# Turned activations laid out sign by sign, in a fused FNet and SoLU kernel on one Trainium2 core

## The chip, the cores and the metric

The kernel runs on one core of one Trainium2 chip. The metric is the device time of one execution in microseconds (us), as a median of several. Before the change it is 1179.93 us (three executions, 1179.46 to 1180.57 us). The profile comes from one execution more, whose span from first to last instruction is 1174.4 us.

Five engines work beside each other: TensorE (PE in the profile; its weight loads are PEld), VectorE (DVE), ScalarE (ACT), GpSimd (POOL) and SyncE (SP), which here does nothing but issue DMA transfers. All tiles named below lie in SBUF with 128 partitions, but for those with `ps` in their name, which lie in PSUM. All arithmetic is in fp32.

## The reference

Eight sequences of 3136 tokens with 256 features go through a two-dimensional Fourier transform, of which the real part is kept. Its rows then go through a feed-forward block with 1024 hidden features.

```python
def _attn_ref(x):                       # x: 8 x 3136 x 256
    X = np.fft.fft(x, axis=1)
    X = np.fft.fft(X, axis=2)
    return X.real.astype(np.float32)

def _moe_ref(x, w_in, w_out, g_ln):     # x: 25088 x 256
    h = x @ w_in                        # 25088 x 1024
    e = np.exp(h - np.max(h, axis=-1, keepdims=True))
    sm = e / (np.sum(e, axis=-1, keepdims=True) + 1e-09)
    solu = h * sm
    mu = np.mean(solu, axis=-1, keepdims=True)
    var = np.mean((solu - mu) ** 2, axis=-1, keepdims=True)
    ln = (solu - mu) / np.sqrt(var + 1e-06) * g_ln
    return ln @ w_out                   # 25088 x 256
```

## The kernel before

The transform over tokens is split as 3136 = 49 x 64. The eight sequences are taken as four pairs, and a pair gives 25 **units**, one for each `k1`. A unit holds 128 tokens of each of two **signs** (`s` = 0 and 1; the tokens of one sign mirror those of the other, and `k1` = 0 has one sign alone). So there are 100 units, numbered 0 to 99.

A unit goes through these steps. `transform2` makes `q` on TensorE, and ScalarE copies it to SBUF. `spread` takes one row of `q` as a column `r`, by a small DMA. `up` multiplies `q` by the weights into PSUM, `even` (VectorE, reads `r`) and `join` make the hidden rows of both signs, and `expo`, `product` and `square` make `u`, which is 128 tokens x 1024 features for each sign. `u` must be transposed, because in the last product its features lie along the partitions. For units 0 to 3 TensorE does that (`turn_whole`). For all later ones VectorE transposes blocks of 32 x 32 into `v` (`turn_blocks`), and DMA moves the blocks to their places in `uT` (`move_blocks`): 16 transfers for two units together, each from 32 partitions to 32 partitions. `down` multiplies `uT` by `Wo`, where 128 x 128 of `uT` are the weights that TensorE loads. For odd units seven products of half-size blocks replace the eight (`Down`, `sums`, `product7`); their sums `S` come from GpSimd. The DMA of the results to `out` ends the unit.

```python
qpool = ctx.enter_context(tc.tile_pool(name="qpool", bufs=4))          # q
...
def spread(t):
    t.r = small.tile([P, 1], FP32, tag="r", name="r")
    nc.sync.dma_start(out=t.r, in_=t.q[0:1, P : 2 * P])
...
class Batch:                            # two units: w = 0 and 1
    def __init__(self, by_blocks):
        if by_blocks:
            self.v = fpool.tile([P, 2, FF, 2], FP32, tag="v", name="v32", bufs=2)
        self.uT = fpool.tile([P, 2, KF, 4, 64], FP32, tag="uT", name="uT", bufs=2)

def turn_blocks(t, s):
    for o in (s,) if len(t.signs) == 2 else (0, 1):
        nc.vector.transpose(out=t.batch.v[:, t.w, :, o], in_=t.u[s])
...
def move_blocks(batch, units, engines=(nc.sync,)):
    v = batch.v[:, units].rearrange("p w (c q n) s -> p q (w c) (n s)", q=4, n=32)
    uT = batch.uT[:, units].rearrange("p w c i m -> p i (w c) m")
    for i in range(4):
        for q in range(4):
            a, b = slice(32 * i, 32 * i + 32), slice(32 * q, 32 * q + 32)
            engines[i % len(engines)].dma_start(out=uT[b, i], in_=v[a, q])
...
def blocks(t):                          # the four blocks of the seven products
    uT = t.batch.uT[:, t.w].rearrange("p c i (n s) -> p s c (i n)", s=2)
    return [uT[:, s, c : c + KF // 2] for s in range(2) for c in (0, KF // 2)]
...
def product7(o, a, b, start=False):
    n = KF // 2
    for c in range(n):
        nc.tensor.matmul(o, a[:, c], b[:, c], start=start and c == 0, stop=c == n - 1, ...)
...
def down(t, s, ps=None):                # the plain product of one sign
    uT = t.batch.uT[:, t.w].rearrange("p c i (n s) -> p c (i n) s", s=2)
    ...
    for c in range(KF):
        nc.tensor.matmul(ps, uT[:, c, :, s], Wo[:, c, :], start=(c == 0), stop=(c == KF - 1))
```

In `v` and `uT` the two signs of a token stand side by side: the value of sign 0, then that of sign 1. A row of 32 tokens of both signs is a run of 64 values, which is 256 bytes, and every reader of one sign steps over the other.

The loop over units, cut to what the change touches. Sums and products of unit `i - lag` stand in step `i`, with `lag` = 4 and `whole` = 4:

```python
for i in range(whole + 1, len(units) + lag + 3):
    cur = units[i] ...                  # fills this step
    old = units[i - lag] ...            # is multiplied by Wo in this step
    kept = units[i - lag - 3] ...       # is stored in this step
    if seven: sums(old)
    ...
    for s in kept.signs: store(kept, s)             # sign 0 by SyncE, sign 1 by GpSimd
    ...
    even(cur, up(cur, 0))
    cur.odd = up(cur, 1)
    second_transform(i + 2)                         # transform2, copy to q, spread
    for s in cur.signs: join(cur, s)
    ...                                             # products of old, expo, product, square
    for s in cur.signs: turn_blocks(cur, s)
    if i >= len(units) - 2:
        move_blocks(batches[-1], slice(cur.w, cur.w + 1), (nc.sync, nc.gpsimd) if cur.w else (nc.sync,))
    elif cur.w:
        move_blocks(batches[-1], slice(0, 2))       # once in two steps
    ...
    if cur.p == 0 and i in (5, 8, 11):
        turn(first, (i + 1) // 3)                   # loads g, which transform2 reads
    for pr in pairs[1:]:
        turn_parts(pr, i - pr.p * NK)               # the same for the next pair
```

Of the kernel before, what the change touches and what calls it, by code (L numbers as in the profile page):

```python
# [9 lines left out]
FP32 = mybir.dt.float32  # L10
# [7 lines left out]
P = 128  # L18
# [17 lines left out]
def kernel(  # L36
# [19 lines left out]
    nc = tc.nc  # L56
    B, S, D = x.shape
    FF = moe_w_in.shape[1]
    KF = FF // P
# [9 lines left out]
    xpool = ctx.enter_context(tc.tile_pool(name="xpool", bufs=2))  # L69
    zpool = ctx.enter_context(tc.tile_pool(name="zpool", bufs=2))  # L70
    gpool = ctx.enter_context(tc.tile_pool(name="gpool", bufs=3))
    qpool = ctx.enter_context(tc.tile_pool(name="qpool", bufs=4))
    small = ctx.enter_context(tc.tile_pool(name="small", bufs=7))
    dram = ctx.enter_context(tc.tile_pool(name="dram", bufs=2, space=bass.MemoryType.DRAM))
    ps_h = ctx.enter_context(tc.tile_pool(name="ps_h", bufs=1, space=PSUM))
# [8 lines left out]
    Wo = const.tile([P, KF, D], FP32, name="Wo")  # L84
# [208 lines left out]
    class Batch:  # L293


        def __init__(self, by_blocks):
            if by_blocks:
                self.v = fpool.tile([P, 2, FF, 2], FP32, tag="v", name="v32", bufs=2)
            self.uT = fpool.tile([P, 2, KF, 4, 64], FP32, tag="uT", name="uT", bufs=2)

    def turn_blocks(t, s):

        for o in (s,) if len(t.signs) == 2 else (0, 1):
            nc.vector.transpose(out=t.batch.v[:, t.w, :, o], in_=t.u[s])  # L304

    def turn_whole(t):

        uT = t.batch.uT[:, t.w].rearrange("p c i (n s) -> p c (i n) s", s=2)
        n = KF // 2
        t.wait = []  # L310
        for s in t.signs:
            for half in range(2):
                ps = result(2 * s + half + 1).rearrange("p (c k) -> p c k", c=n)
                for c in range(n):
                    f = half * n + c
                    nc.tensor.matmul(ps[:, c, :], t.u[s][:, f * P : (f + 1) * P], ident, is_transpose=True,
                                     start=(c == 0), stop=(c == n - 1), skip_group_check=True)
                if s:
                    t.wait.append((uT[:, half * n : (half + 1) * n, :, s], ps))
                else:  # L320
                    nc.scalar.copy(uT[:, half * n : (half + 1) * n, :, s], ps)  # L321

    def move_blocks(batch, units, engines=(nc.sync,)):

        v = batch.v[:, units].rearrange("p w (c q n) s -> p q (w c) (n s)", q=4, n=32)
        uT = batch.uT[:, units].rearrange("p w c i m -> p i (w c) m")
        for i in range(4):
            for q in range(4):
                a, b = slice(32 * i, 32 * i + 32), slice(32 * q, 32 * q + 32)
                engines[i % len(engines)].dma_start(out=uT[b, i], in_=v[a, q])  # L330
# [11 lines left out]
            nc.gpsimd.tensor_tensor(out=Ws[:, j], in0=a, in1=b, op=ALU.subtract)  # L342

    def blocks(t):
        uT = t.batch.uT[:, t.w].rearrange("p c i (n s) -> p s c (i n)", s=2)
        return [uT[:, s, c : c + KF // 2] for s in range(2) for c in (0, KF // 2)]

    def sums(t):

# [86 lines left out]

    def down(t, s, ps=None):

        uT = t.batch.uT[:, t.w].rearrange("p c i (n s) -> p c (i n) s", s=2)
        if ps is None:  # L440
            ps = (result(0) if s else bank(0))[:, 0:D]
        for c in range(KF):
            nc.tensor.matmul(ps, uT[:, c, :, s], Wo[:, c, :], start=(c == 0), stop=(c == KF - 1))  # L443
        return ps

    def scale(t, s, ps):
# [188 lines left out]

    def turn_parts(pr, step):

        at = (-4 if pr.p == 1 else -5, -3, 2, 6, 11)
        if step in at:
            turn(pr, at.index(step))  # L640

    with tc.manual_schedule():
# [102 lines left out]
        def other_pairs(i, do, *a):  # L745
            cur = units[i]
            if cur.p + 1 < NP:
                do(pairs[cur.p + 1], i, *a)
# [3 lines left out]
        for i in range(whole + 1):  # L752
            cur = units[i]
            prv = units[i - 1] if i else None
            if prv:
                turn_whole(prv)
            for s in cur.signs:
                join(cur, s)
            if prv:
                for o, ps in prv.wait:  # L760
                    nc.vector.tensor_copy(out=o, in_=ps)
            for s in cur.signs:
                expo(cur, s)
            if i == whole:
                ps_o = down(units[0], 0)
            if i == 0:

                weights.narrow_out(3)
            for s in cur.signs:
                product(cur, s)  # L770
                if i < whole and s == 0:
                    square(cur, s)
            if i == 1:
                weights.centre()
                weight_sums()
            if i < whole:

                begin(i + 1)
                if 1 in cur.signs:
                    square(cur, 1)  # L780
                stats(cur)
                power(cur)
            else:
                for s in cur.signs:
                    square(cur, s)
                    turn_blocks(cur, s)
                stats(cur)
                power(cur)
                scale(units[0], 0, ps_o)
            if i == 0:  # L790
                turn(first, 1, nc.sync)
            other_pairs(i, ahead)

        def by_seven(i):
# [6 lines left out]
        for i in range(whole + 1, len(units) + lag + 3):  # L801
            cur = units[i] if i < len(units) else None
            old = units[i - lag] if i < len(units) + lag else None
            seven = old and by_seven(i - lag)
            plain, late, scaled = late, None, []
            kept = units[i - lag - 3] if i > whole + 2 else None

            if seven:
                sums(old)
            if fresh:  # L810
                power(fresh)
            fresh = cur
            if kept:
                for s in kept.signs:
                    store(kept, s)
            if done:
                done.finish()
                done = None
            if cur:
                enter(i)  # L820
                even(cur, up(cur, 0))
                cur.odd = up(cur, 1)
                second_transform(i + 2)
                for s in cur.signs:
                    join(cur, s)
            if seven:
                new = Down(old, i == whole + 1)
                new.p1()
                new.seed()
            if half:  # L830
                half.p5()
                half.keep5()
                half.p6()
            if cur:
                expo(cur, 0)
            if half:
                half.keep6()
            if cur:
                if 1 in cur.signs:
                    expo(cur, 1)  # L840
                other_pairs(i, ahead_pe, 0)
            if plain:
                ps_o = down(*plain)
                if not cur:
                    scale(*plain, ps_o)
                    plain = None
            if seven:
                new.p4()
                new.p2()
            elif old is units[-1]:  # L850
                for s in (1, 0):
                    scaled.append((old, s, down(old, s, bank(2 * s)[:, 0:D])))
            elif old:
                scaled.append((old, 0, down(old, 0)))
                late = (old, 1) if 1 in old.signs else None
            if half:
                half.p3()
                half.p7()
                half, done = None, half
            if cur:  # L860
                for s in cur.signs:
                    product(cur, s)
                square(cur, 0)
            if plain:
                scale(*plain, ps_o)
            if seven:
                new.keep4()
                new.keep11()
                half = new
            if cur:  # L870
                if 1 in cur.signs:
                    square(cur, 1)
                other_pairs(i, ahead_pe, 1)
                for s in cur.signs:
                    turn_blocks(cur, s)
# [3 lines that stand above are left out]
                    move_blocks(batches[-1], slice(0, 2))  # L879
                stats(cur)  # L880
            for t, s, ps_o in scaled:
                scale(t, s, ps_o)
            if cur:
                if cur.p == 0 and i in (5, 8, 11):
                    turn(first, (i + 1) // 3)
                for pr in pairs[1:]:
                    turn_parts(pr, i - pr.p * NK)
                other_pairs(i, ahead)
# [76 lines left out]
```

## Time and profile before

| | |
|---|---|
| time, median of 3 | 1179.93 us |
| span of the profiled execution | 1174.4 us |
| PE busy | 1132.6 us, 96% |
| DVE busy | 1005.7 us, 86% |
| ACT busy | 762.4 us, 65% |
| POOL busy | 598.2 us, 51% |
| packets of SyncE's DMA queue | 444608, 146.22 MB |
| transfers `uT<-v` by SyncE | 752 of 128 KB, 24 of 64 KB |

A line of the page on instruction groups gives the source line, the engine, the operation, the tiles (result `<-` operands), the count, the busy time in us, the mean duration in ns, and the time that the engine stood idle just before with what ended it. The page on DMA gives packets, bytes and the share of the 16 DMA engines' time that the packets took. For SyncE a transfer's duration is the time to issue it and not the time in which the bytes move. Engines work beside each other, so busy times don't add up to the span.

### The profile page before, as it was taken

Reading aid. Unit: us, or ns where it says so; the run is one execution under the profiler, and the core shown is the slowest. Engines: PE = TensorE matmul, PEld = TensorE weight load, DVE = VectorE, ACT = ScalarE, POOL = GpSimd, SP = SyncE. Lnnn points to the kernel's source line nnn. Section 1 sums busy time; section 2 is a strip of 40 time slices with the busy share of each in tenths; the row PEclk is TensorE's granted clock in tenths of the full one; section 3 lists DMA queues with packets and bytes.
Section 4 is the critical chain, followed back from the end, with each engine's and each line's share of the span. In section 5 each row is a group of like instructions: output and inputs, shape, how many; then the busy total and the mean of one; then the engine's idle time right before and its main releaser. Section 6 shows DMA issues by size and latency. Waiting matters only on the chain. (4 is left out here: it accounts for less than half of the span.)

```text
span 1174.4 us, 18577 instructions
## 1 busy us (share of the span) xinstructions
PE 1132.6 (96%) x5850; PEld 881.2 (75%) x5850; DVE 1005.7 (86%) x1376; ACT 762.4 (65%) x1841; POOL 598.2 (51%) x558
## 2 busy tenths in 40 slices
PE   2988999999999999999999999999999999999997
PEld 1556787777877787877877777778777787778787
DVE  7789999998878999998879999999887898888870
ACT  4577666757756766767656666676666676677651
POOL 3036666563465566563556666554544334433444
PEclk9999999999999999999999999999999999999999
DMA  9672998865988998865879898865775565745553
GB/s 243 196 186 71 180 183 180 176 141 127 180 185 167 182 167 186 176 141 135 176 146 188 176 188 183 172 146 133 153 154 135 135 152 125 154 108 137 130 116 109
DMA packets 458465, 185.55 MB, mean 158 GB/s; under 512 B 425750, under 2 KB 440350, under 8 KB 458368
## 3 DMA queue, kind: packets, MB, share of 16 engines
q1 hardware_dynamic: 444608, 146.22, 60.4%
q0 software_dynamic: 13760, 38.16, 12.4%
q8 instruction: 47, 0.77, 0.3%
q14 instruction: 50, 0.41, 0.1%
HBM read 44.78 MB, written 38.80 MB: 71 GB/s over the span
## 5 line engine op out<-in xcount | busy, mean ns | idle before, releaser
L443 PE MATMUL ps_m<-Wo,uT 128*128 128x256 f32 x1632 | 369.2, 380 | 3.1 <-ACT uT L321 2.1
L238 PE MATMUL ps_h<-Wi,q 128*128 128x512 f32 x800 | 360.8, 593 | 3.0 <-DVE nmax L252 2.1
L443 PEld LDWEIGHTS ps_m<-Wo,uT 128*128 128x128 f32 x1632 | 314.2, 196 | 33.8 <-ACT uT L321 2.4
L268 DVE SCALAR_TENSOR_TENSOR u<-h,u 128x1024 f32<-128x1024 f32 x196 | 266.1, 1366 | 50.5 <-ACT u L261 36.1
L238 PEld LDWEIGHTS ps_h<-Wi,q 128*128 128x128 f32 x800 | 145.9, 190 | 149.9 <-issue 140.0
L275 ACT ACTIVATE h<-u,usum 128x1024 f32<-128x1024 f32 x196 | 224.4, 1145 | 34.3 <-DVE u L268 33.0
L354 POOL TENSOR_TENSOR S<-uT 128x512 f32<-128x512 f32 x94 | 130.4, 1387 | 208.5 <-issue 138.7
L261 ACT ACTIVATE u<-h,neg 128x1024 f32<-128x1024 f32 x196 | 225.3, 1150 | 6.4
L304 DVE STREAM_TRANSPOSE v<-u 128x1024 f32<-128x1024 f32 x192 | 227.8, 1226 | 0.1
L291 POOL TENSOR_TENSOR rs<-v,neg_half 128x2 f32<-128x2 f32 (+1 forms) x100 | 71.7, 717 | 251.8 <-ACT v L284 251.7
L252 DVE CUSTOM_DVE_ANT_0 h<-ev,ps_h 128x1024 f32<-128x1024 f32 x100 | 122.2, 1222 | 33.3 <-PE ps_h L238 23.5
L244 DVE SCALAR_TENSOR_TENSOR ev<-w_mid,r,ps_h 128x1024 f32<-128x1024 f32 x100 | 126.7, 1267 | 25.6 <-PE ps_h L238 20.6
L359 PE MATMUL ps_m<-Ws,S 128*128 128x128 f32 x1128 | 141.5, 275 | 1.8 <-ACT ot L390 1.8
L216 ACT COPY q<-ps_m 128x256 f32<-128x256 f32 x100 | 36.8, 368 | 159.4 <-PE ps_m L210 155.9
L359 PEld LDWEIGHTS ps_m<-Ws,S 128*128 128x128 f32 x1128 | 133.6, 192 | 2.7 <-issue 1.6
L252 DVE CUSTOM_DVE_ANT_0 h<-h,ps_h 128x1024 f32<-128x1024 f32 x96 | 117.3, 1221 | 13.8
L454 POOL DMA_INDIRECT out_dram<-ot,idx x96 | 100.8, 1050 | 30.7 <-issue 18.7
L359 PE MATMUL ps_m<-Wo,uT 128*128 128x128 f32 x752 | 104.2, 282 | 0.1
L182 PE MATMUL ps_m<-y,F 98*100 98x258 f32 (+3 forms) x288 | 73.4, 390 | 24.7 <-DVE y L130 21.8
L210 PEld LDWEIGHTS ps_m<-T,g 128*128 128x128 f32 x400 | 60.2, 191 | 49.1 <-issue 41.7
L359 PEld LDWEIGHTS ps_m<-Wo,uT 128*128 128x128 f32 x752 | 96.1, 196 | 0.9 <-issue 0.5
L259 ACT ACTIVATE neg<-nmax 128x1 f32<-128x1 f32 x196 | 38.4, 196 | 81.5 <-DVE nmax L252 73.6
(87 smaller groups left out, 1186.7 us busy)
## 6 DMA issues: line engine op xcount, KB each, us to landing
uT<-v SPq DMA_DIRECT2D x752, 128.0 KB
out_dram<-ot SPq DMA_DIRECT2D x100, 128.0 KB
g<-zd POOLq DMA_DIRECT2D x72, 160.0 KB, 5.6
xa<-in_x_dram SPq DMA_DIRECT2D x28, 392.0 KB
zd<-z SPq DMA_DIRECT2D x24, 400.0 KB
raw_in<-in_moe_w_in_dram SPq DMA_DIRECT2D x4, 512.0 KB
raw_out<-in_moe_w_out_dram SPq DMA_DIRECT2D x2, 1024.0 KB
r<-q SPq DMA_DIRECT2D x100, 0.5 KB
```

What stands on the lines that cost most here:

```text
L182: nc.tensor.matmul(o[..., cs], F[:, 2 * t + h, :], i[..., cs], start=first, stop=True, skip_group_check=True)
L238: nc.tensor.matmul(ps[:, fs], t.q[:, c * P : (c + 1) * P], Wi[:, c, fs], start=True, stop=True)
L244: nc.vector.scalar_tensor_tensor(out=t.ev, in0=w_mid, scalar=t.r, in1=ps, op0=ALU.mult, op1=ALU.add)
L252: nc.vector.tensor_tensor_reduce(out=t.h[s], in0=t.h[0] if s else t.ev, in1=t.odd, scale=1.0 if s else -0.5, scalar=-3.0e38, op0=ALU.add, ...
L261: nc.scalar.activation(out=t.u[s], in_=t.h[s], func=ACT.Exp, bias=t.neg[:, s : s + 1], accum_out=t.esum[:, s : s + 1])
L268: nc.vector.scalar_tensor_tensor(out=t.u[s], in0=t.h[s], scalar=1.0, in1=t.u[s], op0=ALU.mult, op1=ALU.mult, accum_out=t.usum[:, s : s + 1])
L275: nc.scalar.activation(out=t.h[s], in_=t.u[s], func=ACT.Square, bias=t.usum[:, s : s + 1], scale=-float(FF), accum_out=t.ssq[:, s : s + 1])
L304: nc.vector.transpose(out=t.batch.v[:, t.w, :, o], in_=t.u[s])
L354: nc.gpsimd.tensor_tensor(out=t.S[:, j], in0=a, in1=b, op=op)
L359: nc.tensor.matmul(o, a[:, c], b[:, c], start=start and c == 0, stop=c == n - 1, skip_group_check=True)
L443: nc.tensor.matmul(ps, uT[:, c, :, s], Wo[:, c, :], start=(c == 0), stop=(c == KF - 1))
L454: dma = nc.gpsimd.indirect_dma_start(out=out, out_offset=bass.IndirectOffsetOnAxis(ap=idx[:, i : i + 1], axis=0), in_=t.ot[s], in_offset=None)
```

## The change

The two signs no longer stand side by side. `v` and `uT` become `[P, 2, KF, 2, P]`, with the 128 tokens of one sign together, so that each reader of one sign reads neighbouring values: the weight loads of `down` and `product7`, the sums on GpSimd, the copies of `turn_whole`; and `transpose` writes neighbouring values. The runs that the block moves carry are then 32 tokens of one sign, 128 bytes. The bytes and the number of transfers stay the same.

`r` and `q` of a unit are made three units ahead instead of two, which takes a fifth buffer for `q`; the loads of `g`, which `transform2` reads, are moved one step ahead with them. That gives the small DMA of `r`, which stands in the same queue as the block moves, more time.

```diff
-    qpool = ctx.enter_context(tc.tile_pool(name="qpool", bufs=4))
+    qpool = ctx.enter_context(tc.tile_pool(name="qpool", bufs=5))
...
-                self.v = fpool.tile([P, 2, FF, 2], FP32, tag="v", name="v32", bufs=2)
-            self.uT = fpool.tile([P, 2, KF, 4, 64], FP32, tag="uT", name="uT", bufs=2)
+                self.v = fpool.tile([P, 2, KF, 2, P], FP32, tag="v", name="v32", bufs=2)
+            self.uT = fpool.tile([P, 2, KF, 2, P], FP32, tag="uT", name="uT", bufs=2)
...
-            nc.vector.transpose(out=t.batch.v[:, t.w, :, o], in_=t.u[s])
+            nc.vector.transpose(out=t.batch.v[:, t.w, :, o, :], in_=t.u[s].rearrange("p (c k) -> p c k", c=KF))
...
-        v = batch.v[:, units].rearrange("p w (c q n) s -> p q (w c) (n s)", q=4, n=32)
-        uT = batch.uT[:, units].rearrange("p w c i m -> p i (w c) m")
+        v = batch.v[:, units].rearrange("p w c s (q n) -> p q (w c s) n", q=4)
+        uT = batch.uT[:, units].rearrange("p w c s (i n) -> p i (w c s) n", i=4)
...
-        uT = t.batch.uT[:, t.w].rearrange("p c i (n s) -> p s c (i n)", s=2)
-        return [uT[:, s, c : c + KF // 2] for s in range(2) for c in (0, KF // 2)]
+        return [t.batch.uT[:, t.w, c : c + KF // 2, s, :] for s in range(2) for c in (0, KF // 2)]
...
-            nc.tensor.matmul(ps, uT[:, c, :, s], Wo[:, c, :], start=(c == 0), stop=(c == KF - 1))
+            nc.tensor.matmul(ps, uT[:, c, s, :], Wo[:, c, :], start=(c == 0), stop=(c == KF - 1))
...
-        at = (-4 if pr.p == 1 else -5, -3, 2, 6, 11)
+        at = (-5, -3, 2, 6, 11)
...
+            if i == whole:
+                turn(first, 2)
...
-                second_transform(i + 2)
+                for j in (2, 3) if i == whole + 1 else (3,):
+                    second_transform(i + j)
...
-                if cur.p == 0 and i in (5, 8, 11):
-                    turn(first, (i + 1) // 3)
+                if i in (7, 10):
+                    turn(first, (i + 2) // 3)
```

More of the change, by code (lines that the diff above doesn't have):

```diff
@@ L297, in __init__ @@
             if by_blocks:
-                self.v = fpool.tile([P, 2, FF, 2], FP32, tag="v", name="v32", bufs=2)
-            self.uT = fpool.tile([P, 2, KF, 4, 64], FP32, tag="uT", name="uT", bufs=2)
+                self.v = fpool.tile([P, 2, KF, 2, P], FP32, tag="v", name="v32", bufs=2)
+            self.uT = fpool.tile([P, 2, KF, 2, P], FP32, tag="uT", name="uT", bufs=2)
     def turn_blocks(t, s):
         for o in (s,) if len(t.signs) == 2 else (0, 1):
-            nc.vector.transpose(out=t.batch.v[:, t.w, :, o], in_=t.u[s])
+            nc.vector.transpose(out=t.batch.v[:, t.w, :, o, :], in_=t.u[s].rearrange("p (c k) -> p c k", c=KF))
     def turn_whole(t):
-        uT = t.batch.uT[:, t.w].rearrange("p c i (n s) -> p c (i n) s", s=2)
+        uT = t.batch.uT[:, t.w]
         n = KF // 2
@@ L318, in turn_whole @@
                 if s:
-                    t.wait.append((uT[:, half * n : (half + 1) * n, :, s], ps))
+                    t.wait.append((uT[:, half * n : (half + 1) * n, s, :], ps))
                 else:
-                    nc.scalar.copy(uT[:, half * n : (half + 1) * n, :, s], ps)
+                    nc.scalar.copy(uT[:, half * n : (half + 1) * n, s, :], ps)
     def move_blocks(batch, units, engines=(nc.sync,)):
-        v = batch.v[:, units].rearrange("p w (c q n) s -> p q (w c) (n s)", q=4, n=32)
-        uT = batch.uT[:, units].rearrange("p w c i m -> p i (w c) m")
+        v = batch.v[:, units].rearrange("p w c s (q n) -> p q (w c s) n", q=4)
+        uT = batch.uT[:, units].rearrange("p w c s (i n) -> p i (w c s) n", i=4)
         for i in range(4):
@@ L437, in down @@
     def down(t, s, ps=None):
-        uT = t.batch.uT[:, t.w].rearrange("p c i (n s) -> p c (i n) s", s=2)
+        uT = t.batch.uT[:, t.w]
         if ps is None:
```

## The prediction

> **What bounds the kernel now.** I read the busy shares first, then the groups of instructions of the whole span, then the waits of TensorE, and then the DMA by short stretches. The page says that TensorE is busy for 96% of the span:
>
> ```profile
> PE 1132.6 (96%) x5850; PEld 881.2 (75%) x5850; DVE 1005.7 (86%) x1376; ACT 762.4 (65%) x1841; POOL 598.2 (51%) x558
> ...
> L443 PE MATMUL ps_m<-Wo,uT 128*128 128x256 f32 x1632 | 369.2, 380 | 3.1 <-ACT uT L321 2.1
> ...
> q1 hardware_dynamic: 444608, 146.22, 60.4%
> ...
> uT<-v SPq DMA_DIRECT2D x752, 128.0 KB
> ```
>
> The missing 4% lie before 94 us; from 100 us to 1150 us TensorE's matmuls start one behind the other, and the gaps over 0.15 us sum to some 7 us. So TensorE sets the pace: the block moves of two successive pairs of units start at 1076.32 and 1097.07 us, 20.75 us apart, and over the whole loop (111.9 to 1118.1 us, 46 steps) 21.9 us apart. A saving counts only where TensorE saves, and a delay only if something else needs more than 21.9 us for two units. The one candidate is the queue of SyncE, with 60.4% of the DMA engines' time, so I looked at it in a quiet stretch near the end, where no loads for a next pair are under way. The timeline of SyncE for two units:
>
> ```profile
> 1076.32 12.98 SPq L330 DMA_DIRECT2D uT<-v  x16
> 1089.35 0.79 SPq L458 DMA_DIRECT2D out_dram<-ot  x1
> 1090.23 0.82 SPq L221 DMA_DIRECT2D r<-q  x1
> 1091.10 0.59 SPq L458 DMA_DIRECT2D out_dram<-ot  x1
> 1091.78 1.25 SPq L221 DMA_DIRECT2D r<-q  x1
> 1097.07 3.61 SPq L330 DMA_DIRECT2D uT<-v  x5
> ```
>
> The first column is the start, the second the length. Sixteen moves and four small transfers fill 16.7 us of the 20.75. And the DMA view of 4.0 us, from 1086.5 to 1090.5 us, in which the queue holds block moves and nothing else:
>
> ```profile
> DMA packets 2466, 0.61 MB, mean 153 GB/s; under 512 B 2466, under 2 KB 2466, under 8 KB 2466
> ...
> q1 hardware_dynamic: 2466, 0.61, 67.5%
> ```
>
> 2466 packets in 4.0 us are 617 a microsecond, some of them the small closing ones of each transfer; without those it is 600, or 1.67 ns for each run of 256 bytes. Yet the 16 engines are busy for only 67.5% of it. They wait for work a third of the time. For 0.6 us from 1084.7 us, with a backlog, they moved 213 GB/s with a share of 97.0%. In the packet records the starts of the steady stretch recur every 27 ns: one packet to each of 16 engines in 26.7 ns, though a packet takes 18 ns. So neither the bytes nor the engines set this pace, but whatever hands out the runs, one by one. The isolated transfers of `r` near 56 us support it: 128 runs of 4 bytes need 0.41 us, or 3.2 ns each, no less than runs of 256 bytes.
>
> **What the Trainium skill says.** "Perfetto Trace Analysis", section "DMA Instruction — HWDGE (DVE, Sync)", says that one block generates the descriptors of a DMA that SyncE issues, that it is held for one DMA at a time, and that the profiler's window of such an instruction doesn't contain the movement. The trace agrees that issue and movement are apart: first issues last 0.64 us, later ones up to 1.2 us, while the packets of each need 512 x 1.67 = 0.85 us. "DMA: Bandwidth & Descriptors", section "Why small descriptors are slow (HBM only)", says that transfers within SBUF don't suffer from small descriptors, and that 128-byte packets still reach 78% of the link. That speaks for a harmless change. The trace speaks against it: 153 GB/s with 256 bytes and idle engines. No run so far has 128 bytes. For the strided reads, "SBUF — State Buffer", section "Door 1: The DMA port swizzle (why `[64,N]` ≈ `[32,N]`)", has lines of 16 bytes within which a step is free, so every second fp32 should cost nothing. The trace almost agrees, as the next part shows.
>
> **What the change removes on TensorE.** From one weight-load group to the next:
>
> ```profile
> 602.01 1.87 PEld L359 LDWEIGHTS ps_m<-Ws,S 128*128 128x128 f32 x16
> 603.80 3.34 PEld L443 LDWEIGHTS ps_m<-Wo,uT 128*128 128x128 f32 x16
> ...
> 612.92 1.02 PEld L359 LDWEIGHTS ps_m<-Wo,uT 128*128 128x128 f32 x8
> 613.87 3.34 PEld L443 LDWEIGHTS ps_m<-Wo,uT 128*128 128x128 f32 x16
> ```
>
> Packed `S`: 1.79 us for 16, 112 ns each. Every second value of `uT`: 0.95 us for 8, 118 ns each. The seven products have 752 + 376 = 1128 matmuls with `uT` as weights, so 1128 x 6 ns = 6.8 us could go. The 1632 matmuls with 256 columns follow every 216 ns, and those of line 607, with packed `ones` as weights, every 216 ns too: nothing to gain. So TensorE saves 6.8 us, 0.6% of the time.
>
> **On the other engines.** The transposes (1.23 us each, 192) may get a little shorter with a packed result, and the sums on GpSimd (1.3 to 1.5 us) too. Neither engine sets the pace. Three units ahead costs no work at all: as many transforms, one buffer more. Waits for `r` are small now (VectorE 2.8 us in all), so it is there for a fuller queue.
>
> **What it adds.** A block move has 32 partitions x 16 runs = 512 runs now, and 32 x 32 = 1024 afterwards. If each run costs 1.67 ns whatever its length, a move needs 1.71 us, and sixteen 27.3 us. Beside them stand, in the same queue, two `r` of 0.41 us and two results of 128 runs of 1 KB (8 for each engine at 46 ns, 0.37 us): 1.6 us. That makes 28.9 us, against 21.9 us that TensorE needs. The queue becomes the bound. Its slack doesn't help: `uT` and `v` have two buffers each, so the lag of four units can absorb a late transfer, but not a rate.
>
> The sum: first moves at 111.9 us; 47 pairs x 28.9 = 1358 us; the two last units, 24 moves of 512 runs through SyncE, 24 x 0.85 = 20 us; from the last move (1154.1) to the end 20.3 us; and 5.5 us that the median lies above the profile. That is 1516 us. The sixteen moves are issued in 12.98 us, so with the bursts a move takes 0.81 instead of 0.85 us; at that pace 47 x (26.0 + 1.6) = 1297 us and 1455 us in all. I take 1490 us, between them. TensorE's 6.8 us disappear in its idle time.
>
> **The rivals.**
> - *The moves stay hidden.* If the pace were one of bytes, 16 moves would keep their 13 to 17 us, TensorE would stay the bound, and the time would be 1180 - 7 = 1173 us, perhaps up to 1190 with a busier queue in the stretches with loads. For it: the page on descriptors, and that somebody moved the transforms ahead, as if a small delay had to be covered. Against it: engines idle for a third of the time at 600 runs a microsecond.
> - *A packet has a fixed part and a part by bytes.* From 256 to 1024 bytes a packet grows from 18 to 46 ns, 0.0365 ns a byte. Of 26.7 ns between starts on one engine, 9.3 are then bytes; 128 bytes would need 17.4 + 4.7 = 22 ns, a move 64 x 22 = 1.41 us, two units 22.5 + 1.6 = 24.1 us. 47 x 24.1 + 112 + 20 + 20 + 5.5 gives 1290 us. For it: a smooth law. Against it: the backlog, where the engines took 256 bytes every 18.6 ns.
> - *Worse than the pace.* The stores of `zd` and the loads of `xa` stand in the same queue, and `g` waits for `zd`. With a queue that is always late, `g` may come late when a pair ends, three times, some 10 to 20 us each: up to 1560 us.
>
> **Range and chances.** I give the pace by runs about three in four, the mixed law and the hidden moves the rest in about equal parts. 1290 to 1570 us holds the first, its worse form and most of the second. Faster by over 2% would need over 23 us, three times what TensorE saves: 0.02. Within 2%: 0.12. Slower by over 2%: 0.86.
>
> **What would show it.** Right: the DMA view of a steady stretch has about 600 packets of 128 bytes a microsecond, near 77 GB/s, at a lower share of the engines than 67%; SyncE's sixteen issues last 25 to 28 us and follow one another without waiting for `v`; TensorE idles about 7 us in every two units, ended by `uT`; line 359 with `uT` follows every 112 ns. Wrong: more than 900 packets a microsecond, or sixteen issues in less than 20 us with TensorE still without gaps.

## The result and the profile after

The changed kernel takes 1222.35 us (median of 6 runs, 1217.23 to 1227.07), the kernel before 1179.7 us beside it: a ratio of 1.036, with an interval of 1.033 to 1.040. It is slower, as predicted, but by 43 us and not by 310. The profiled execution has a span of 1224.2 us, 49.8 us more than before.

The lines of the page that answer to those shown of before:

```profile
PE 1143.2 (93%) x5850; PEld 874.2 (71%) x5850; DVE 1012.0 (83%) x1376; ACT 762.4 (62%) x1841; POOL 600.7 (49%) x558
...
L442 PE MATMUL ps_m<-Wo,uT 128*128 128x256 f32 x1632 | 382.0, 389 | 33.7 <-DMA uT<-v 10.6
...
q1 hardware_dynamic: 835776, 146.22, 80.3%
...
uT<-v SPq DMA_DIRECT2D x752, 128.0 KB
```

The packets of SyncE's queue almost double for the same bytes, and its share goes from 60.4% of 1174.4 us to 80.3% of 1224.2: 39% more engine time. The product with `uT` now stands idle for 33.7 us instead of 3.1.

The timeline of SyncE for two units, late in the run, where nothing is loaded for a next pair (start, length):

```profile
1105.47 15.91 SPq L330 DMA_DIRECT2D uT<-v  x16
1121.42 0.70 SPq L457 DMA_DIRECT2D out_dram<-ot  x1
1122.24 0.97 SPq L221 DMA_DIRECT2D r<-q  x1
1123.26 0.83 SPq L457 DMA_DIRECT2D out_dram<-ot  x1
1124.19 0.53 SPq L221 DMA_DIRECT2D r<-q  x1
1126.40 3.96 SPq L330 DMA_DIRECT2D uT<-v  x5
```

Sixteen moves take 15.9 us instead of 13.0, yet the next ones start 20.93 us later, so the queue is in time. The DMA view of 1110 to 1120 us, inside these moves (packets, MB, share):

```profile
q1 hardware_dynamic: 9669, 1.22, 101.8%
```

That is 967 runs a microsecond at full engines; a share over 100% comes from packets whose recorded times overlap. And while a next pair's data comes in, SyncE looks like this:

```profile
762.21 21.77 SPq L330 DMA_DIRECT2D uT<-v  x16
784.02 1.24 SPq L457 DMA_DIRECT2D out_dram<-ot  x1
785.36 0.99 SPq L221 DMA_DIRECT2D r<-q  x1
786.44 0.51 SPq L190 DMA_DIRECT2D zd<-z  x1
787.05 0.35 SPq L115 DMA_DIRECT2D xa<-in_x_dram  x1
787.45 0.61 SPq L457 DMA_DIRECT2D out_dram<-ot  x1
788.16 2.27 SPq L221 DMA_DIRECT2D r<-q  x1
790.59 1.37 SPq L330 DMA_DIRECT2D uT<-v  x2
```

Here `xa` is a part of the next pair's input (`xb`, loaded by GpSimd, is the other), and `zd` is the result of its first transform on the way to DRAM, from where `g` is loaded. The moves alone need 21.8 us and the next begin 28.4 us later: TensorE's 21.9 us are overrun. Over the first 31 pairs of units the sixteen moves are issued in 18.3 us on average (14.5 before), over the last 12 in 15.8 (13.2 before).

Engine busy times by 100 us of the run show where it hurts (columns: PE, PEld, DVE, ACT, POOL busy, granted clock, DMA share, GB/s):

```profile
200.00:300.00 100.00, 99.03 (x532) 77.37 (x531) 93.22 (x118) 67.93 (x167) 42.87 (x36) 1.00 1.03 150
300.00:400.00 100.00, 90.71 (x449) 69.35 (x447) 72.79 (x100) 55.41 (x139) 57.58 (x56) 0.95 0.93 151
400.00:500.00 100.00, 90.60 (x468) 69.06 (x468) 90.66 (x113) 67.02 (x163) 60.21 (x52) 1.00 1.04 164
...
700.00:800.00 100.00, 88.92 (x436) 66.47 (x435) 84.53 (x108) 60.52 (x149) 55.38 (x50) 0.95 0.97 164
800.00:900.00 100.00, 99.94 (x536) 77.76 (x535) 90.15 (x117) 67.72 (x167) 48.37 (x45) 1.00 0.99 149
...
1000.00:1100.00 100.00, 100.00 (x534) 77.42 (x533) 85.52 (x120) 68.27 (x168) 42.82 (x42) 1.00 0.92 137
```

TensorE loses about 10% of some stretches before 800 us and next to nothing after, though the DMA share is above 0.9 in all of them. In the kernel before it was busy for 98.0 us or more of each of these stretches. The last loads of the last pair are issued at 810 us and its last store of `zd` at 876 us (754 and 820 us before). What TensorE waited for, from the view of waits (total us, times, longest):

```profile
PE ps_m L442 <- DMA uT<-v: 10.6, 3, 5.5
PE ps_m L442 <- DMA out_dram<-ot: 10.0, 5, 3.4
PE ps_m L442 <- DMA r<-q: 9.2, 2, 7.8
PE ps_m L210 <- DMA g<-zd: 6.9, 1, 6.9
```

Every one is a transfer. The transfers of SyncE share their semaphores, and the view names the one that was issued last; line 442 reads only `uT` and `Wo`, so where it is said to wait for `out_dram` or `r`, the block moves of `uT` are what it needs. I also took the intervals between successive matmul starts of the trace and subtracted the usual interval of each kind. From 100 to 800 us the excess is about 61 us (8 before), later about 3 us (1 before): some 55 us more.

It has two parts. After 110 us TensorE's recorded idle time grows from 4.8 to 43.7 us: +38.9. Most of the rest is the clock. The weight loads of TensorE's lines 442 and 358 near 600 us:

```profile
603.86 0.97 PEld L358 LDWEIGHTS ps_m<-Wo,uT 128*128 128x128 f32 x8
604.75 3.33 PEld L442 LDWEIGHTS ps_m<-Wo,uT 128*128 128x128 f32 x16
...
619.34 6.27 PEld L442 LDWEIGHTS ps_m<-Wo,uT 128*128 128x128 f32 x16 [3.60 <-ACT u L261]
```

The same sixteen take 3.33 us, and 6.27 us after a wait of 3.60 us. The engine view of the stretch from 618.5 us has 0.51 as its granted clock:

```profile
618.50:625.40 6.90, 6.03 (x14) 4.88 (x15) 3.48 (x4) 2.97 (x7) 0.00 (x0) 0.51 0.79 130
```

The clock records have seven such stretches at half clock before the last matmul, 41 us in all; the trace of before has none there. Matmuls that started in them without a wait lost some 13 us. The Trainium skill, "TensorE: Matmul & The Clock Gate", section "Part 1: The HAM clock gate (the "warmup" mystery)", says that the clock falls to one half after an idle window of about 3.4 us. This trace agrees on the window and not on how idle it has to be: all seven stretches start on one grid of 3.41 us, but the window just before each holds 2.1 to 3.4 us of idle time between recorded matmuls, and windows with up to 1.76 us were not followed by a fall. Over all traces of this kernel and its variants, from 60 us on, 70 falls followed windows with 1.74 us of idle time or more and none followed a window with less; up to 1.95 us it did not always fall. So a wait of some 2 us can be enough. With a first matmul that came 3.2 us later (at 20.0 us; in run 9, whose start is that of the kernel before, it comes at 21.8, so I don't put this down to the change) and the saving of 6.8 us, the sum is 55 + 3.2 - 6.8 = 51 us, against 49.8 measured.

The saving itself is in the first two lines above: 0.89 us from one group of 8 to the next, 111 ns each.

### The profile page after: what moved, and what is told of

It is laid out like the page before. It is cut to its first block, busy times and chain, and to the rows that moved or that the text cites. A ratio compares the mean times of both kernels' runs of the same rounds, so it can differ in the third digit from the quotient of the medians.

```text
span 1224.2 us, 18574 instructions
## 1 busy us (share of the span) xinstructions
PE 1143.2 (93%) x5850; PEld 874.2 (71%) x5850; DVE 1012.0 (83%) x1376; ACT 762.4 (62%) x1841; POOL 600.7 (49%) x558
## 3 DMA queue, kind: packets, MB, share of 16 engines
q1 hardware_dynamic: 835776, 146.22, 80.3%
## 5 line engine op out<-in xcount | busy, mean ns | idle before, releaser
L442 PE MATMUL ps_m<-Wo,uT 128*128 128x256 f32 x1632 | 382.0, 389 | 33.7 <-DMA uT<-v 10.6
L442 PEld LDWEIGHTS ps_m<-Wo,uT 128*128 128x128 f32 x1632 | 312.1, 196 | 80.7 <-issue 17.8
L268 DVE SCALAR_TENSOR_TENSOR u<-h,u 128x1024 f32<-128x1024 f32 x196 | 277.0, 1422 | 59.1 <-ACT u L261 48.6
L291 POOL TENSOR_TENSOR rs<-v,neg_half 128x2 f32<-128x2 f32 (+1 forms) x100 | 76.8, 768 | 231.5 <-ACT v L284 231.4
L358 PE MATMUL ps_m<-Wo,uT 128*128 128x128 f32 x752 | 99.4, 275 | 0.1
L358 PEld LDWEIGHTS ps_m<-Wo,uT 128*128 128x128 f32 x752 | 91.7, 192 | 1.3 <-issue 1.0
L389 ACT ACTIVATE ot<-ps_m,rs 128x128 f32<-128x128 f32 x188 | 64.8, 359 | 32.4 <-PE ps_m L358 27.0
```

The costliest lines, as they stand in the source:

```text
L268: nc.vector.scalar_tensor_tensor(out=t.u[s], in0=t.h[s], scalar=1.0, in1=t.u[s], op0=ALU.mult, op1=ALU.mult, accum_out=t.usum[:, s : s + 1])
L291: nc.gpsimd.tensor_tensor(out=t.rs[:, n], in0=t.v[:, n], in1=neg_half[:, n], op=ALU.pow)
L442: nc.tensor.matmul(ps, uT[:, c, s, :], Wo[:, c, :], start=(c == 0), stop=(c == KF - 1))
```

## The experiments

Ratios are to the kernel before, run on the same chip, with their intervals.

| | us | ratio |
|---|---|---|
| the change | 1222.35 | 1.036 (1.033 to 1.040) |
| 1 layout alone | 1223.49 | 1.042 (1.038 to 1.046) |
| 2 three ahead alone | 1183.52 | 1.0056 (1.0042 to 1.0071) |
| 3 the change, few loads | 1188.69 | 1.0083 (1.0060 to 1.0106) |
| 5 layout in units 68 to 99 | 1180.28 | 1.0018 (1.0008 to 1.0028) |
| 6 layout in units 4 to 67 | 1225.31 | 1.038 (1.034 to 1.041) |
| 7 moves in two queues | 1688.09 | 1.433 (1.430 to 1.435) |
| 8 before, few loads | 1184.28 | 1.0050 (1.0032 to 1.0068) |
| 9 as 5, then three ahead | 1175.07 | 0.9975 (0.9966 to 0.9985) |
| 10 runs of 512 bytes | 1336.29 | 1.135 (1.133 to 1.136) |

Runs 4, 11 and 12 measure transfers by themselves and have no ratio. The theory at the start of the runs: the moves are not paced by runs; they and the loads share the engines, and only beside loads do they come too late. The rival is the prediction's own, a constant time for each run.

### 1 and 2: the two parts alone

Run 1 is the changed kernel without the third unit ahead, with the turns of before:

```diff
-    qpool = ctx.enter_context(tc.tile_pool(name="qpool", bufs=5))
+    qpool = ctx.enter_context(tc.tile_pool(name="qpool", bufs=4))
...
-                for j in (2, 3) if i == whole + 1 else (3,):
-                    second_transform(i + j)
+                second_transform(i + 2)
```

> The new layout with its 128-byte runs, but the second transform two units ahead as before. If full DMA engines are the cause, the layout alone loses at least what the change loses: 1215 to 1250 us, with some waits for r on top. If the order in SyncE's queue is the cause (r, zd and xa behind the block moves), r is late in nearly every second unit and the loss is far larger than the change's, over 1250 us.

Run 2 is the kernel before with that part of the change alone.

> The layout of before with its 256-byte runs, and the second transform three units ahead. Under either theory this does no more work and waits for nothing new: 1174 to 1183 us. If three units ahead costs something by itself (g needed one unit earlier), 1190 us or more, and the layout would be to blame for less than the whole loss.

The layout alone costs 4.2%, three ahead alone 0.6%, and both together 3.6%. What three ahead does for the new layout is in VectorE's waits of run 1:

```profile
DVE ev L244 <- DMA r<-q: 77.8, 28, 8.2
```

In the changed kernel this wait is gone, yet that brought back only some 0.6%, in ratios whose intervals overlap a little. TensorE's own waits show what took its place: those ended by a transfer, after 110 us, are 15.1 us in run 1 and 36.6 us in the changed kernel. Where `r` no longer holds the units back, `uT` does. Without the layout, three ahead has nothing to remove (2.8 us), and one late load of `g` costs TensorE 3.8 us.

### 3 and 8: few loads

In run 3 the loads of pairs 1 to 3 fetch one token row of 1 KB for each partition instead of the four rows of each of two tiles (`xa`, and `xb` by an indirect transfer); the sums of all four rows are then formed from that one. It leaves out 16.9 MB of 185.6 MB of transfers, so its results are not the reference's. Everything else stays.

```diff
+        if pr.p:
+            nc.sync.dma_start(out=xb[:, 0:1], in_=x_pn[r, c * CH + 1 : c * CH + 2, :])
+        else:
             nc.sync.dma_start(out=xa, in_=x_pn[r, c * CH + 1 : (c + 1) * CH + 1, :])
             nc.gpsimd.indirect_dma_start(out=xb ...)
```

> The changed kernel, but the pairs 1 to 3 load one row of 98 x 1 KB in place of 98 x 4 KB plus as much again by indirect DMA, and form their sums from that row, with the same engine work (their results are then not the reference's). If full DMA engines are the cause, TensorE's gaps go down with the traffic: 1175 to 1200 us. If the order in SyncE's queue is the cause, the number of its transfers stays the same and so does the time: 1210 us or more.

Run 8 is its control: the same edit in the kernel before.

> The control for the light loads: the kernel before with the same small loads for pairs 1 to 3. TensorE is the bound there, so less traffic brings little under either theory: 1165 to 1180 us. The gap between this and the changed kernel with light loads (1188.7 us) is what 128-byte runs still cost without the loads: 5 to 15 us if full engines explain the change; 40 us or so if they don't.

With all loads the layouts are 43 us apart; with few loads 1188.69 - 1184.28 = 4.4 us. The block moves are the same in number, bytes and run length. So 128-byte runs don't set a rate of their own over the loop; nine tenths of the loss needs the loads beside them. Which loads, those in the moves' own queue (`xa`) or GpSimd's (`xb`), these two runs don't separate. (The edit itself makes the kernel before 0.5% slower; by what, I did not follow up.)

### 4: the pace of the moves by themselves

A probe with transfers alone: 32 moves of 128 KB for each run length, from 32 to 32 partitions as in the kernel, then from two queues, then within the same partitions, then over all 128 partitions. All computation is left out.

```python
src = v.rearrange("p (r q n) -> p q r n", q=4, n=words)
for t in uT:
    dst = t.rearrange("p (r i n) -> p i r n", i=4, n=words)
    for i in range(4):
        for q in range(4):
            nc.sync.dma_start(out=dst[32*q : 32*q+32, i], in_=src[32*i : 32*i+32, q])
```

> No reference work at all, only DMA: 32 moves of 128 KB from 32 partitions to 32 partitions for each of the run lengths 64, 128, 256, 512 and 1024 bytes through SyncE, then 128 and 256 through SyncE and ScalarE in turn, then within the same partitions, then 128 partitions wide; zeros are stored at the end. If a packet costs a fixed part and a part by bytes (2 to 3 ns and 0.092 ns a byte on one engine, from the steady stretches before and after), 16 moves need about 27 us at 64 bytes (a floor of 13 ns), 15 us at 128, 13.7 us at 256, 13 us at 512. If each run costs 1.67 ns whatever its length, 64: 55 us, 128: 27 us, 512: 7 us. If the pace at 256 bytes is a limit of one queue, two queues bring it to 10 us (213 GB/s); if it is a limit of the partitions read and written, two queues bring nothing and the wide transfers bring up to twice the rate.

| run | runs per us, 32 partitions | GB/s | ns per packet and engine | runs per us, 128 partitions | GB/s |
|---|---|---|---|---|---|
| 64 B | 1530 | 98 | 10.5 | | |
| 128 B | 1390 | 178 | 11.5 | 1610 | 206 |
| 256 B | 745 | 191 | 21.5 | 835 | 214 |
| 512 B | 385 | 197 | 41.6 | | |
| 1 KB | 198 | 203 | 80.8 | 330 | 335 |

The DMA view inside the phase of 128-byte runs, 64 to 80 us:

```profile
DMA packets 22545, 2.84 MB, mean 178 GB/s; under 512 B 22545, under 2 KB 22545, under 8 KB 22545
...
q1 hardware_dynamic: 22545, 2.84, 106.3%
```

22545 in 16 us are 1409 a microsecond, where the prediction had 600 for any length. From 128 bytes up, twice the length is nearly twice the time: these narrow moves are paced by bytes, near 200 GB/s, and 64-byte runs show a floor of some 10.5 ns a packet, which 128 bytes almost reach. Sixteen moves take, by these paces, 21.4 us with 64 bytes, 11.8 with 128, 11.0 with 256 and 10.6 with 512: somewhat less than the first law expected, and far from a constant time for each run. From two queues 128-byte moves reached up to 215 GB/s, 256-byte ones gained nothing. What does grow with short runs is work for the engines: a packet holds its engine for 13 ns by its record (median) instead of 18, and there are twice as many, so 26 ns for the same bytes.

### 5 and 6: the layout in part of the run

The kernel before, with the new layout for some units only; a flag of the batch chooses the shapes of `v` and `uT`.

```diff
-                batches.append(Batch(i >= whole))
+                batches.append(Batch(i >= whole, i >= 68))               # run 5
+                batches.append(Batch(i >= whole, whole <= i < 68))       # run 6
```

> The kernel before, with the new layout for units 68 to 99 alone, whose moves run after the last loads of a next pair; the second transform stays two units ahead. If DMA engines that are full through the loads are the cause, the new layout costs nothing there and TensorE keeps its saving of 6 ns for each of the 16 x 24 = 384 matmuls: 2.3 us less than before, 1173 to 1178 us, ratio 0.998. If 128-byte runs cost time wherever they stand (r late, issue order), a third of the loss of the layout alone comes back: some 15 us more, 1190 us or above.

> The kernel before, with the new layout for units 4 to 67 alone, the rest in the old one; two units ahead. If the loads' traffic is the cause, this carries the whole loss of the layout alone, 1218 to 1230 us. If the loss is spread over all units, two thirds of it: 1205 to 1212 us.

In the last 32 units, where no pair is loaded, the layout costs 0.2%; in the 64 before them all but a tenth of what it costs everywhere (3.8 of 4.2%). With run 3 this is the same answer by another way: place and presence of loads agree.

### 7: the moves from two queues

```diff
-                    move_blocks(batches[-1], slice(0, 2))
+                    move_blocks(batches[-1], slice(0, 2), (nc.sync, nc.scalar))
```

> The changed kernel, with the sixteen moves issued by SyncE and ScalarE in turn. If SyncE's one queue is what holds the moves back (its transfers stand behind each other), half of the moves get past the loads and stores there and TensorE's waits for uT shrink: 1180 to 1205 us, less what ScalarE pays for eight issues of some 0.6 us in two units. If the DMA engines themselves are full, the moves gain nothing and ScalarE loses: 1220 us or more.

ScalarE's timeline, with its next instruction:

```profile
628.61 11.64 ACTq L330 DMA_DIRECT2D uT<-v  x8
640.30 0.29 ACT L282 ACTIVATE es<-esum,limits 128x2 f32<-128x2 f32 x1 [11.91 <-issue]
```

The two queues together issue the sixteen in 12.9 us, but ScalarE stands still while it issues its eight, and VectorE then waits 520 us in all for ScalarE's `u`. The run says nothing on queue against engines; it shows only what it costs to let a computing engine issue long transfers.

### 9: the layout where it does not hurt

Run 5, with three units ahead from step 67 on.

```diff
-    qpool = ctx.enter_context(tc.tile_pool(name="qpool", bufs=4))
+    qpool = ctx.enter_context(tc.tile_pool(name="qpool", bufs=5))
...
-                second_transform(i + 2)
+                for j in (2,) if i < 67 else (2, 3) if i == 67 else (3,):
+                    second_transform(i + j)
```

> As the packed layout for units 68 to 99 alone, with the second transform three units ahead from step 67 on. If what that run lost was the wait for r behind the longer moves (15.8 us on VectorE), it goes, and TensorE's saving is left: 2.3 us under before, 1174 to 1177 us. If the moves themselves still cost something without loads, it stays at 1179 us or more.

1175.07 us, 2.8 us less than before beside it, and faster than both kernels. The expected saving was a third of TensorE's 6.8 us. Run 5 alone lost it again: VectorE waited for `r` there 7 times, 15.8 us in all, after 790 us. In run 9 no such wait is left after 790 us. So both parts of the change do what they are for, once the queue has time.

### 10: longer runs instead

The other way round: both units and both signs of a batch interleaved, runs of 512 bytes, and readers that step over four values (16 bytes), for units 4 to 97.

```diff
+                self.v = fpool.tile([P, FF, 2, 2] ...)
+            self.uT = fpool.tile([P, KF, P, 2, 2] ...)
...
+            v = batch.v.rearrange("p (c q n) w s -> p q c (n w s)", q=4, n=32)
+            uT = batch.uT.rearrange("p c (i n) w s -> p i c (n w s)", i=4)
```

> The kernel before with both units and both signs of a token side by side in v and uT for units 4 to 97: runs of 512 bytes, read by every fourth fp32. If full DMA engines are what the change suffers from, 512-byte runs leave them emptier than before and the waits for DMA fall, but before had only some 8 us of them; TensorE's loads of uT with a step of 16 bytes cost as much as with 8 (118 ns) or more. So 1172 to 1180 us if the step costs nothing more, 1185 us and above if each of 1100 loads goes to 125 ns or the plain products pay too.

From its groups by shape (busy us, mean ns, idle before):

```profile
L456 PEld LDWEIGHTS ps_m<-Wo,uT 128*128 128x128 f32 x1632 | 384.5, 320 | 7.0 <-ACT uT L325 2.4 <-ACT q L216 1.3
L306 DVE STREAM_TRANSPOSE v<-u 128x1024 f32<-128x1024 f32 x188 | 372.3, 2063 | 0.1
...
L369 PE MATMUL ps_m<-Wo,uT 128*128 128x128 f32 x752 | 187.1, 392 | 1.1 <-ACT ot L461 1.1
...
L364 POOL TENSOR_TENSOR S<-uT 128x512 f32<-128x512 f32 x94 | 161.2, 1715 | 268.7 <-issue 168.7 <-PE ps_m L369 91.5 <-DMA uT<-v 8.4
```

The queue's share falls to 49%, and after 100 us no recorded wait of TensorE ends with it. But a weight load takes 320 ns instead of 196, so 128-column matmuls follow every 233 ns instead of 118 and 256-column ones every 233 instead of 216; a transpose takes 2063 ns instead of 1226. TensorE is busy for 97% of a longer span, and its matmuls account for the loss: 1128 x 115 ns + 1632 x 17 ns = 157 us, of 158 measured. The expectation had a few ns for each load. The Trainium skill, "SBUF — State Buffer", section "Door 1: The DMA port swizzle (why `[64,N]` ≈ `[32,N]`)", which the prediction cited for lines of 16 bytes, fits: a step of 8 bytes is almost free, 118 against 112 ns, and one of 16 bytes, a value to each line, isn't (233 ns). The section also says that one can stride over 4 fp32 for free; for a step of four, run 10 shows the contrary.

### 11 and 12: the moves beside other work

Run 11 was to set moves of 256 and of 128 bytes beside VectorE, ScalarE, TensorE and loads in turn, with nothing computed that the reference asks for.

> Only DMA and idle work beside it: 32 moves each of 256-byte and of 128-byte runs, first alone (745 and 1390 runs a microsecond in the first such run), then beside VectorE, ScalarE, TensorE, all three, then beside eight loads of 392 KB, then all together. If the kernel's slower pace (600 runs of 256 bytes a microsecond, 1070 of 128) comes from engines that use the same SBUF, it shows beside one or all of them; if not, all stay at 745 and 1390. Beside loads: if packets fill the engines, 128-byte moves with loads need over 1.2 times as long as 256-byte moves with loads; if bytes alone count, the same within a tenth.

Its plan failed in part. Only VectorE's additions were tied to their phases; ScalarE's copies ran from 18 to 83 us, TensorE's matmuls from 17 to 277 us, and the loads without a tie to any phase, while the moves stood still from 39 to 91 us for a reason that I didn't find. What it does show: beside VectorE's additions and beside TensorE's matmuls the moves keep 728 to 748 and 1377 to 1389 runs a microsecond. Run 12 has the loads alone, tied to their phases:

```python
for loads in (0, 2, 4, 8, 0):
    for words in (64, 32):               # runs of 256 and of 128 bytes
        ...                              # the loads wait for the phase before
        for k in range(loads):           # 392 KB each, packets of 4 KB
            nc.scalar.dma_start(out=ld[k], in_=x_pn[...])
        phase(words, [nc.sync])          # the 32 moves of run 4
```

> A probe with transfers alone: 32 moves of 128 KB by SyncE from 32 to 32 partitions, once in runs of 256 bytes and once in runs of 128 bytes, beside 0, 2, 4 and 8 loads of 392 KB from HBM in packets of 4 KB, which ScalarE issues as the moves begin. Alone the moves should repeat 745 and 1390 runs a microsecond, 22 and 23.6 us for the 32. Theory (moves and loads share the engines' time by bytes, and 128-byte runs hold an engine longer a byte): each load takes about 1.2 to 1.9 us from the moves, so beside 8 loads the 32 moves need 32 to 37 us with runs of 256 bytes, and with runs of 128 bytes 3 to 10 us more than that, the difference growing with the number of loads. Rival 1 (loads and moves alternate packet by packet on an engine): beside a load every move packet waits for a 4 KB packet, so the pace in packets falls to about the same for both lengths, well under 300 a microsecond, and the 128-byte moves get half the bytes while loads last. Rival 2 (loads stop the moves, whatever the runs): both lengths are late by the same time, 11 to 12 us beside 8 loads, and the pace falls under 150 runs a microsecond for both; then what hurts in the kernel is not a worse sharing but that the moves of 128 bytes have less slack to give.

A phase ends when VectorE may clear `uT` again. The timeline of VectorE, where the time in brackets is that of the 32 moves from release to clearing:

```profile
46.01 3.47 DVE L65 MEMSET uT<- 128x4096 f32 x1 [24.74 <-issue]
...
80.00 3.47 DVE L65 MEMSET uT<- 128x4096 f32 x1 [26.12 <-issue]
...
278.85 3.47 DVE L65 MEMSET uT<- 128x4096 f32 x1 [37.18 <-issue]
...
325.02 3.47 DVE L65 MEMSET uT<- 128x4096 f32 x1 [38.31 <-issue]
```

In pairs, 256 then 128 bytes, beside no load and beside eight. By the packets themselves the 32 moves last 22.1 and 23.7 us beside no load, 25.3 and 27.3 beside two, 28.5 and 30.2 beside four, 34.4 and 35.5 beside eight. Each load delays either kind by 1.5 to 1.8 us, and 128-byte runs are 1.2 to 2.0 us later whatever stands beside them. While eight loads ran, 256-byte runs went at 206 a microsecond and 128-byte ones at 350 (53 and 45 GB/s), the loads at 183 and 196 GB/s; after them both came back to their full pace. So the first theory is wrong on one point: the short runs don't share worse beside loads. Its figures for 256 bytes hold (34 us), its growing difference doesn't. Rival 1 falls, since the two paces differ by far; rival 2 has the equal delay right, though not a pace under 150. What is left is slack: the loads take the same from both, and the new layout has less to give.

## Why the prediction was wrong, step by step

- **TensorE bounds before; a delay counts only beyond 21.9 us for two units.** Right. It is why the new layout is harmless in quiet stretches and in run 5.
- **TensorE saves 6.8 us.** Right: 112 ns instead of 118, and nothing with 256 columns (216 ns). Run 9 shows its third.
- **"If each run costs 1.67 ns whatever its length".** This is the step that failed, and with it the 28.9 us for two units and the three times of 1455 to 1516 us. Run 4 has 0.72 ns a run for 128 bytes and 0.65 for 64. The 1.67 ns were the mean of a stretch with idle engines, and I took the idleness as proof of a limit in the handing-out of runs. The same trace held the counter-evidence: for 0.6 us the engines took 213 GB/s, 830 runs a microsecond, which no floor of 1.67 ns allows. Nor do the 3.2 ns for each run of `r` give a pace of runs in general, since run 4 moves runs of 64 bytes in 0.65 ns; what made `r` slow, no run shows.
- **The queue becomes the bound, everywhere.** It became one in places. When quiet, the sixteen moves went from 13.2 to 15.8 us, not to 27.3, and with the 3.7 us of the others in the queue they fit into 21 us. Beside loads (sets with over 0.4 MB of packets of 4 KB under way) they went from 15.2 to 19.0 us on average. With 3.7 us for the others, one of 24 such sets overran 21.9 us before, and 16 of 27 after. Then `uT`, `r` and results are late together.
- **What should show it.** Of the four signs only the 112 ns came. 967 runs a microsecond instead of 600, 122 GB/s instead of 77, 101.8% of the engines instead of under 67%, and sixteen issues in under 20 us in a quiet stretch: the prediction's own sign for wrong, over 900, was met.
- **The rivals.** "The moves stay hidden" holds after 800 us and with few loads (1188.69 us, inside its 1173 to 1190), and fails beside loads. "A fixed part and a part by bytes" named the kind of law that run 4 shows from 128 bytes up, but with a fixed part far too large: 17.4 ns, where 11.5 and 80.8 ns for 128 bytes and 1 KB leave under 2. Its 22 ns a packet were 11.5 alone and some 16 in the kernel. "Worse than the pace" didn't come, apart from one wait of 6.9 us for `g`.
- **Not in the prediction.** The half clock after waits, some 13 us.

Open: in the kernel the moves run slower than by themselves, about 617 against 750 runs a microsecond with 256 bytes and 967 against 1409 with 128, so that the new layout costs two to three us for sixteen moves there and only 0.8 us (half of 23.7 - 22.1) alone. VectorE's additions and TensorE's matmuls are not the cause by run 11, and for 256 bytes neither are ScalarE's copies, beside which its first moves kept 748 a microsecond (24 to 39 us). GpSimd's sums and the kernel's own stores weren't separated. Nor is it shown why loads widen the difference between the layouts in the kernel (sixteen moves 2.6 us apart in the last 12 pairs, 3.8 us beside loads), when run 12 has no such growth.

## What to carry to other kernels

A mean pace in a stretch where the engines idle is not a limit; look for the fastest stretch of the trace before building a law on it, and time the same transfer by itself at two sizes. A transfer that stays behind a bound engine has a slack in each period, and what a change costs it must be added up where the queue is fullest, here beside the loads of the next pair, not in the quiet stretch where it is easiest to read. A layout can also be changed only where the queue has time: run 9 keeps the gain and avoids the loss.

## What the runs showed of the hardware

- Moves from 32 to 32 partitions stay near 200 GB/s at any run length of 256 bytes to 1 KB (191 to 203); over 128 partitions 1 KB runs reach 335 GB/s, but 128-byte runs only 206.
- A wait of 3.6 us for a transfer cost TensorE nearly as much again: the next sixteen weight loads took 6.27 instead of 3.33 us. In these traces the clock fell to one half 70 times, always after a window of 3.41 us of which TensorE was idle for 1.74 us or more.
- Loads in 4 KB packets take about three quarters of the bytes while they run, 183 of 236 GB/s, from a move queue that alone reaches 191.
- A step of 8 bytes lengthens a weight load by 4 ns at most (196 against 192 to 196 ns) and the interval of 128-column matmuls by 6 ns; one of 16 bytes lengthens the load by 124 ns and that interval by 121; a transpose that writes with a step of 16 bytes takes 2063 instead of 1226 ns, one with 8 bytes 1226 against 1220.
- ScalarE was held for 11.6 us by eight moves that it issued.
